# Attention and token/channel mixer on one core: first keys by another queue, a weight ordered by another engine, and a reordered fourth step

## The chip, the core and the metric

The kernel runs on one core of a Trainium2 chip. The core has a matrix engine (TensorE, PE in the profile), a vector engine (VectorE, DVE), a scalar engine (ScalarE, ACT), a general engine (GpSimd, POOL) and a queue engine (SyncE, SP) that here only issues transfers. Each works through its own instructions in the order in which the program lists them, and waits on semaphores where an instruction needs another engine's result. Matmul results go to PSUM, from which VectorE or ScalarE must copy them ("evacuate") to SBUF before they can be used again.

The metric is the device time of one execution in microseconds. A kernel is timed in several runs and the median is compared.

## What is computed

Eight batches of twelve attention heads with 448 tokens and 64 values a head, then a mixer over tokens and one over channels:

```python
scores = scale * np.matmul(q, k.transpose(0, 1, 3, 2))
attn = np.maximum(scores, 0.0) ** 2 / S
x = matmul(attn, v)            # heads joined: (8, 448, 768)
h = np.maximum(x.T @ w_tok1, 0.0) @ w_tok2      # over tokens
u = x + h.T
h2 = np.maximum(u @ w_ch1, 0.0) @ w_ch2         # over channels
out = u + h2
```

Inputs and output are float32. Inside, the kernel works in bf16. The sizes are S = 448, w_tok1 448x256, w_tok2 256x448, w_ch1 768x1536, w_ch2 1536x768.

## The kernel before

**Tiling.** Four heads make a step, so a batch is three steps (DB = 3) and the program has 24 steps (ND = 24). The text calls them step 0, step 1 and so on, by the loop variable i. A step's keys are cut into seven chunks (QC = 7) of 64. All matmuls of scores and values use 64x64 quarters of the array, four at a time.

**One step of attention.** `load_four(i)` (L72) loads queries, keys and values of four heads: two transfers each, issued by GpSimd, which cast from float32 to bf16 on the way. `transposes` (L157) turns queries and keys on TensorE and copies them out as qkT (L181). `scores(i, c)` (L186) makes the scores of a chunk into one of two PSUM tiles, and ScalarE evacuates them with a Relu (L201). `square` (L205) squares them on VectorE (L208). `values(i, cs)` (L210) accumulates the product with the values in ps_acc, which has one tile, and `values_out` (L229) writes it as xT on VectorE (L234).

**Mixer.** `x_back(i)` (L246) turns xT into x_sb: for i below XDMA = 7 by eight TensorE transposes into two PSUM tiles and two VectorE copies (L259, L267), from there on by two DMA transposes issued on SP (L252). `token1` (L271) multiplies by the first token weight, ScalarE evacuates (L284). `token2` (L287) multiplies by the second (L300), and VectorE adds xT into uT (L308). Once a batch has its three steps, `channel_work(b)` (L384) issues the six DMA transposes of `u_back` on SP (L326) and puts units of the channel mixer in a queue: `channel1` is six matmuls and a ScalarE Relu (L338, L345), `channel2` twelve matmuls and a VectorE add (L355, L362), and every second `channel2` unit stores the finished rows (L374). For an even batch the `channel2` units wait until the next batch is done.

**Order.** The program order is written out by hand. The first steps (0 to DB, so 0 to 3) are in a loop over steps and chunks (L432), which places each piece of work after a given chunk. From step 4 on a second loop (L478) is used, and `fill(share)` (L400) takes units from the queue in between: it adds a share of a rate to a credit, and runs units while the credit is above zero, each of which costs its estimated length (C1 = 1134, C2 = 1956). PSUM tiles of the tag "bank" (ps_mm, two of them) are shared by the early transposes, x_back, token1, the early form of token2 and the channel units. In the second loop GpSimd waits by a small copy (`gate`, L493) for x_sb when `i - 1 >= XDMA` before it issues the loads for step i + 3.

**Weights.** All weights are loaded by GpSimd with a cast. The second token weight is loaded in its natural order and rearranged on chip by `order_wt2` (L97): two strided copies of 128x448, one on ScalarE and one on VectorE, placed after chunk 6 of step 1. The first use of it is `token2(0)` in step 2.

**Start.** Nine matmuls on zeros (L417) run while the first loads are on their way. Step 0 has a function of its own for its transposes, `transposes_first` (L121): fourteen transposes for the queries, fourteen for the keys, each 128 partitions high, and copies of their own (L129).

Of the kernel before, what the change touches and what calls it, by code (L numbers as in the profile page):

```python
# [9 lines left out]
FP32 = mybir.dt.float32  # L10
# [6 lines left out]
def kernel(  # L17
# [51 lines left out]


    raws = {}
    def load_four(i):  # L72
        b, d = divmod(i, DB)
        tiles = []
        for name, src in (("q", q), ("k", k), ("v", v)):
            t = raw.tile([128, 2, QC, D], BF16, name=f"{name}_raw")
            for r in range(2):
                h0 = 4 * d + 2 * r
                nc.gpsimd.dma_start(  # L79
                    out=t[64 * r : 64 * (r + 1)].rearrange("p g c d -> p g (c d)"),  # L80
                    in_=src[b, h0 : h0 + 2].rearrange("g (p c) d -> p g (c d)", c=QC),
                )
            tiles.append(t)
        raws[i] = tiles

# [10 lines left out]

    def order_wt2():  # L97
        for j in range(JC):
            (nc.scalar.copy if j == 0 else nc.vector.tensor_copy)(
                wt2[:, j, :].rearrange("n (c p) -> n c p", c=QC),  # L100
                wt2_nat[:, j, :].rearrange("n (p c) -> n c p", c=QC),
            )

    def load_wc1(i, parts):
        n = DC // parts
        nc.gpsimd.dma_start(
            out=wc1[:, :, i * n : (i + 1) * n],
            in_=moe_w_ch1.rearrange("(g p) n -> p g n", p=128)[:, :, i * n : (i + 1) * n],
        )
# [8 lines left out]

    qkT, at2, squares, accs = {}, {}, [], {}

    def transposes_first(i, early=True):  # L121
        sb = attn.tile([128, 2, 2, S], BF16, name="qkT")
        if not early:
            both = ps_acc.tile([128, 2, 1024], BF16, tag="acc", name="qkT_ps")
        def copies(w, ps):
            halves = [slice(0, 2)] if i > 0 or w == 0 else [slice(0, 1), slice(1, 2)]
            for n, r in enumerate(halves):
                on_act = early and (w == 0) == (i > 0) and n == 0
                (nc.scalar.copy if on_act else nc.vector.tensor_copy)(  # L129
                    sb[:, r, w, :].rearrange("n r (c p) -> n r c p", c=QC),  # L130
                    ps[:, : 2 * S].rearrange("n (c r p) -> n r c p", c=QC, r=2)[:, r],
                )

        parts = []
        for w in range(2):
            src = raws[i][w]
            ps = ps_mm.tile([128, 1024], BF16, tag="bank", name="qkT_ps1") if early else both[:, w]
            for c in range(QC):
                for g in range(2):
                    nc.tensor.matmul(  # L140
                        ps[64 * g : 64 * (g + 1), c * 128 : (c + 1) * 128],
                        lhsT=src[:, g, c, :],
                        rhs=ident,
                        is_transpose=True,
                        start=True,
                        stop=True,
                        skip_group_check=True,
                    )
            parts.append(ps)
            if early:  # L150
                copies(w, ps)
        if not early:
            for w in range(2):
                copies(w, parts[w])
        qkT[i] = sb

    def transposes(i, early=False):  # L157
        sb = attn.tile([128, 2, 2, S], BF16, name="qkT")
        if early:
            parts = [ps_mm.tile([128, 1024], BF16, tag="bank", name="qkT_ps1") for r in range(2)]  # L160
        else:
            both = ps_acc.tile([128, 2, 1024], BF16, tag="acc", name="qkT_ps")
            parts = [both[:, r] for r in range(2)]
        for w in range(2):
            src = raws[i][w]
            for c in range(QC):
                at = w * S + c * 64
                for r in range(2):
                    h = slice(64 * r, 64 * (r + 1))
                    for g in range(2):  # L170
                        nc.tensor.matmul(  # L171
                            parts[r][64 * g : 64 * (g + 1), at : at + 64],
                            lhsT=src[h, g, c, :],
                            rhs=ident[h, h],
                            is_transpose=True,
                            start=True,
                            stop=True,
                            skip_group_check=True,
                        )
        for r in range(2):  # L180
            (nc.scalar.copy if early and r == 0 else nc.vector.tensor_copy)(  # L181
                sb[:, r].rearrange("n w t -> n (w t)"), parts[r][:, : 2 * S]
            )
        qkT[i] = sb
# [56 lines left out]


    x_tiles, r1_tiles, uT_tiles = {}, {}, {}
    XDMA = 7

    def x_back(i):  # L246
        b, d = divmod(i, DB)
        x_sb = mix.tile([128, 2, 4, 128], BF16, name="x_sb")
        x_tiles[i] = x_sb
        if i >= XDMA:  # L250
            for r in range(2):
                nc.sync.dma_start_transpose(  # L252
                    out=x_sb[:, r], in_=xT[b % 2][:, 2 * d + r, :]
                )
            return
        for r in range(2):
            ps = ps_mm.tile([128, 1024], BF16, tag="bank", name="x_ps")
            for c in range(4):
                nc.tensor.matmul(  # L259
                    ps[:, c * 128 : (c + 1) * 128],  # L260
                    lhsT=xT[b % 2][:, 2 * d + r, c * 128 : (c + 1) * 128],
                    rhs=ident,
                    is_transpose=True,
                    start=(c == 0),
                    stop=(c == 3),
                )
            nc.vector.tensor_copy(  # L267
                x_sb[:, r], ps[:, :512].rearrange("n (c d) -> n c d", c=4)
            )

    def token1(i):  # L271
        x_sb = x_tiles.pop(i)
# [74 lines left out]
    def channel2(b, t, half):  # L347
# [21 lines left out]
        if half == 1 or last:  # L369
            part = cols if last else slice(0, DM)  # L370
            (b0, c0), (b1, c1) = divmod(2 * t, QC), divmod(2 * t + 1, QC)
            rows = [out[2 * (b // 2) + n].rearrange("(p c) m -> c p m", c=QC) for n in range(2)]
            for k, (n, c) in enumerate(((b0, c0), (b1, c1))):
                nc.sync.dma_start(  # L374
                    out=rows[n][c, :, part], in_=o[64 * k : 64 * (k + 1), part]
                )
        if half == 1:
# [19 lines left out]
    credit = [0.0]  # L397
    rate = [EC * C1 / 3.5]

    def fill(share):  # L400
        if not queue:
            return
        credit[0] += share * rate[0]
        while queue and credit[0] > 0:
            cost, unit = queue.pop(0)
            credit[0] -= cost
            unit()


    PRE = 3  # L410
# [15 lines left out]
    load_wt2()  # L426
    load_four(3)
    load_wc1(0, 2)


    transposes_first(0)
    for i in range(DB + 1):  # L432
        for c in range(QC):
            scores(i, c)
            square(keep=1)
            if c < 3 and i > 0:
                values(i - 1, (4 + c,))
                if c == 2:
                    values_out(i - 1)
            if i < DB:  # L440
                if c == 3:
                    transposes(i + 1, early=True)
                if c == 4 and i > 0:
                    x_back(i - 1)
                if c == 5:
                    values(i, (0, 1))
                if c == 6:
                    if i > 0:
                        token1(i - 1)
                    values(i, (2, 3))  # L450
                if c == 0 and i > 1:
                    token2(i - 2, early=True)
                if c == 6 and i == 1:
                    order_wt2()
            else:
                if c == 0:
                    token2(i - 2, early=True)
                if c == 3:
                    x_back(i - 1)
                if c == 4:  # L460
                    transposes(i + 1)
                    token1(i - 1)
                if c == 6:
                    token2(i - 1)
                    channel_work(0)
        if i == 1:
            load_four(4)
            load_wc1(1, 2)
        if i == 2:
            load_four(5)  # L470
            load_wc2(0, 4)
        if i == 3:
            load_four(6)
            load_wc2(1, 4)
    square()
    fill(1 / 2)

    for i in range(DB + 1, ND + 2):  # L478
        if i == 2 * DB + 1:
# [22 lines left out]
        if i + 1 < ND:  # L502
            transposes(i + 1)
        square()
        fill(1 / 6)
        if 0 <= i - 1 < ND:
            token1(i - 1)
        fill(1 / 6)
        if i < ND:
            scores(i, 5)  # L510
            scores(i, 6)
# [38 lines left out]
```

## Time and profile before

The median of 13 runs is 391.26 us (390.13 to 393.53). The profiled execution took 392.82 us, of which 391.0 lie between its first and last instruction (its span).

| what | value |
|---|---|
| median of 13 runs | 391.26 us |
| profiled execution, span | 392.82 us, 391.0 us |
| granted TensorE clock, mean over the span | 0.977 of full speed |
| TensorE, VectorE, ScalarE, GpSimd busy | 367.9, 207.6, 211.6, 97.9 us |
| chain that ended last, by engine | PE 85%, DVE 5%, DMA 4%, ACT 3% |
| scores' evacuation L201 (168 instructions) | 144.7 us, 920 ns each |
| squares L208 (168) | 97.1 us, 617 ns each |
| loads of q, k, v, issue to landing (median) | 4.2, 5.0, 5.1 us |
| DMA transposes of u and of x, issue to landing (median) | 3.9, 2.4 us |

The profile comes from one execution. Busy time of a matmul engine counts pipelined instructions, so it shows where the engine had work rather than how fast it went. The page divides the span into 40 slices of 9.8 us; a digit is the busy share in tenths. A wait is put down to the engine that released it last.

### The profile page before, as it was taken

How to read it: one execution, taken by the hardware profiler on the slowest of the kernel's cores; microseconds unless marked ns; L12 is line 12 of the kernel's file. 1: busy time of each engine (PE TensorE's matmuls, PEld its weight loads, DVE VectorE, ACT ScalarE, POOL GpSimd, SP SyncE). 2: the span in 40 equal slices, each digit the busy share in tenths (PEclk: the TensorE clock that was granted, in tenths of full speed). 3: DMA queues.
4: the chain of work that ended last, by engine and by line, in shares of the span. 5: the costliest groups of instructions: out<-in, count | busy, mean ns of one | idle time of the engine just before them, and what ended most of it. 6: DMA issues, size and time to landing. Idle time of an engine off the chain costs nothing.

```text
span 391.0 us, 9968 instructions
## 1 busy us (share of the span) xinstructions
PE 367.9 (94%) x4261; PEld 201.0 (51%) x4261; DVE 207.6 (53%) x384; ACT 211.6 (54%) x295; POOL 97.9 (25%) x177
## 2 busy tenths in 40 slices
PE   5877899999999799999999999999999999999995
PEld 2443445445555445555555555545545555555563
DVE  1697676764575635645744756645743755221021
ACT  2987667766644245772676445763576445411400
POOL 9963364510304032223033033123120000000000
PEclk8598999999999989999999999999999999999999
DMA  7999999970359585696557977497453423234024
GB/s 108 131 192 175 181 200 184 183 107 2 57 108 168 94 148 110 102 135 123 109 89 103 119 139 137 78 127 134 113 72 69 89 63 89 59 65 107 2 58 103
DMA packets 70957, 43.33 MB, mean 111 GB/s; under 512 B 44992, under 2 KB 67456, under 8 KB 70912
## 3 DMA queue, kind: packets, MB, share of 16 engines
q0 software_dynamic: 24736, 21.70, 39.1%
q1 hardware_dynamic: 46176, 20.99, 28.1%
q8 instruction: 33, 0.54, 0.6%
q14 instruction: 12, 0.10, 0.1%
HBM read 43.38 MB, written 11.01 MB: 139 GB/s over the span
## 4 chain that ended last, share of the span: by engine, by line
PE 85%; DVE 5%; DMA 4%; ACT 3%; issue 1%; POOL 1%; POOLq 0%; ACTq 0%; DVEq 0%
PE m_ps L355 27%; PE m_ps L338 27%; PE sc_ps L192 9%; PE acc_ps L220 8%; PE t_ps L276 6%; PE h_ps L300 5%; DMA x_sb<-xT 3%; DVE xT L234 3%; PE qkT_ps L171 2%; ACT at L201 2%; DVE at L208 2%; DMA k_raw<-in_k_dram 1%; PE x_ps L259 1%; DVE uT_sb L308 1%; ACT r_sb L284 1%
## 5 line engine op out<-in xcount | busy, mean ns | idle before, releaser
L201 ACT ACTIVATE at<-sc_ps 128x896 bf16<-128x896 f32 x168 | 144.7, 920 | 61.2 <-PE sc_ps L192 61.1
L338 PE MATMUL m_ps<-uT_sb,wc 128*128 128x448 bf16 x576 | 117.4, 353 | 0.5 <-DVE uT_sb L308 0.5
L355 PE MATMUL m_ps<-wc,r_sb 128*128 128x384 bf16 x672 | 116.8, 329 | 0.0
L208 DVE TENSOR_TENSOR at<-at 128x896 bf16<-128x896 bf16 x168 | 97.1, 617 | 6.2 <-ACT at L201 6.2
L345 ACT ACTIVATE r_sb<-m_ps 128x448 bf16<-128x448 f32 x96 | 52.2, 543 | 68.9 <-PE m_ps L338 68.2
L355 PEld LDWEIGHTS <-r_sb 128*128 128x128 bf16 x672 | 64.9, 99 | 46.6 <-issue 5.5
L338 PEld LDWEIGHTS <-wc 128*128 128x128 bf16 x576 | 55.0, 98 | 50.9 <-issue 3.4
L362 DVE TENSOR_TENSOR out_sb<-m_ps,u_sb 128x384 f32<-128x384 f32 x56 | 31.0, 553 | 61.7 <-PE m_ps L355 61.7
L192 PE MATMUL sc_ps<-qkT 64*64 64x448 bf16 x672 | 54.4, 373 | 3.0 <-ACT at L201 2.3
L308 DVE TENSOR_TENSOR uT_sb<-h_ps,xT 128x448 bf16<-128x448 f32 x48 | 27.7, 619 | 53.4 <-PE h_ps L300 53.4
L234 DVE TENSOR_SCALAR xT<-acc_ps 128x448 bf16<-128x448 f32 x48 | 27.7, 619 | 32.3 <-PE acc_ps L220 32.3
L493 POOL COPY gate<-x_sb 1x1 bf16<-1x1 bf16 x13 | 2.5, 196 | 148.6 <-DMA x_sb<-xT 148.6
L220 PE MATMUL acc_ps<-at,v_raw 64*64 64x448 bf16 x672 | 39.6, 359 | 0.0
L79 POOL DMA_DIRECT2D q_raw<-in_q_dram x48 | 28.9, 609 | 26.9 <-DMA wc<-in_moe_w_ch_dram 18.6
L181 DVE COPY qkT<-qkT_ps 128x896 bf16<-128x896 bf16 x43 | 24.9, 619 | 17.6 <-PE qkT_ps L171 17.6
L192 PEld LDWEIGHTS <-qkT 64*64 64x64 bf16 x672 | 15.5, 107 | 31.5 <-issue 27.3
L79 POOL DMA_DIRECT2D v_raw<-in_v_dram x48 | 29.4, 635 | 6.1 <-PE sc_ps L192 4.3
L79 POOL DMA_DIRECT2D k_raw<-in_k_dram x48 | 29.1, 623 | 4.2 <-DMA k_raw<-in_k_dram 1.9
L276 PE MATMUL t_ps<-x_sb,wt 128*128 128x256 bf16 x192 | 25.7, 278 | 2.8 <-DMA x_sb<-xT 2.8
L284 ACT ACTIVATE r_sb<-t_ps 128x512 bf16<-128x512 f32 x24 | 14.4, 599 | 22.4 <-PE t_ps L276 22.4
L220 PEld LDWEIGHTS <-v_raw 64*64 64x64 bf16 x672 | 20.1, 109 | 12.5 <-issue 1.2
L300 PE MATMUL h_ps<-wt,r_sb 128*128 128x448 bf16 x96 | 22.3, 355 | 1.7 <-ACT r_sb L284 1.0
(35 smaller groups left out, 103.2 us busy)
## 6 DMA issues: line engine op xcount, KB each, us to landing
out_dram<-out_sb SPq DMA_DIRECT2D x54, 192.0 KB, 2.7
q_raw<-in_q_dram POOLq DMA_DIRECT2D x48, 112.0 KB, 4.2
k_raw<-in_k_dram POOLq DMA_DIRECT2D x48, 112.0 KB, 5.0
v_raw<-in_v_dram POOLq DMA_DIRECT2D x48, 112.0 KB, 5.1
wc<-in_moe_w_ch_dram POOLq DMA_DIRECT2D x2, 1152.0 KB, 14.0
wc<-in_moe_w_ch_dram POOLq DMA_DIRECT2D x4, 576.0 KB, 11.1
u_sb<-uT_sb SPq DMA_TRANSPOSE x48, 3.9
x_sb<-xT SPq DMA_TRANSPOSE x34, 2.4
```

Of the source, the lines that this page charges most:

```text
L79: nc.gpsimd.dma_start(out=t[64 * r : 64 * (r + 1)].rearrange("p g c d -> p g (c d)"), in_=src[b, h0 : h0 + 2].rearrange("g (p c) d -> p g ...
L192: nc.tensor.matmul(ps[64 * r : 64 * (r + 1), g, :S], lhsT=sb[h, r, 1, c * 64 : (c + 1) * 64], rhs=sb[h, r, 0, :], start=True, stop=True, s ...
L201: nc.scalar.activation(at, ps[:, :, :S], AF.Relu)
L208: nc.vector.tensor_tensor(out=at, in0=at, in1=at, op=ALU.mult)
L220: nc.tensor.matmul(ps[64 * g : 64 * (g + 1), r, :S], lhsT=v_raw[h, g, c, :], rhs=at[h, g, :], start=(c == 0), stop=(c == QC - 1), skip_gro ...
L234: nc.vector.tensor_scalar(out=xT[b % 2][:, 2 * d + r, :S], in0=ps[:, r, :S], scalar1=float(alpha2), scalar2=None, op0=ALU.mult,)
L276: nc.tensor.matmul(ps[:, j, :], lhsT=wt1[:, c, j * 128 : (j + 1) * 128], rhs=x_sb[:, :, c, :], start=(c == 0), stop=(c == 3),)
L300: nc.tensor.matmul(parts[r][:, :S], lhsT=r1[:, j, r * 128 : (r + 1) * 128], rhs=wt2[:, j, :], start=(j == 0), stop=(j == JC - 1),)
L308: nc.vector.tensor_tensor(out=uT_tiles[b // 2][:, 2 * d + r, off : off + S], in0=parts[r][:, :S], in1=xT[b % 2][:, 2 * d + r, :S], op=ALU.add,
L338: nc.tensor.matmul(ps[:, :S], lhsT=wc1[:, g, e * 128 : (e + 1) * 128], rhs=uT[:, g, off : off + S], start=(g == 0), stop=(g == CC - 1),)
L345: nc.scalar.activation(r2[:, e, off : off + S], ps[:, :S], AF.Relu)
L355: nc.tensor.matmul(ps[:, :HN], lhsT=r2[:, e, t * 128 : (t + 1) * 128], rhs=wc2[:, e, cols], start=(e == 0), stop=(e == EC - 1),)
```

## The change

The diff has seven parts.

1. For step 0, the two transfers of the keys are issued on SP and on ScalarE's queue instead of GpSimd's, as float32 into a new tile `k_first`. One ScalarE copy and one VectorE copy cast its halves to bf16.
2. `order_wt2` is called after the issue of the first half of the first channel weight, ahead of step 0, and both its copies are on GpSimd.
3. `transposes_first` is gone. Step 0 uses `transposes(0, early=True)`, which turns the keys before the queries for this step. ScalarE copies out one pair of heads (128x896), VectorE the other.
4. `x_back` puts its eight transposes into one PSUM tile, with one copy out of it, and XDMA goes from 7 to 6: step 6's x goes by DMA transposes, and GpSimd's gate begins in step 7.
5. In step 3 (i = DB) the last values of step 2 come ahead of the scores of chunks 0 and 1, and x_back, token1, token2 and the channel work move up by one or two chunks. token2 takes its early form (ps_mm). One `fill(1 / 4)` runs after chunk 5 and one after the loop, instead of one `fill(1 / 2)` after the loop.
6. In the second loop the shares around token1 are 2/9 and 1/9 instead of 1/6 and 1/6, and the second takes at least one unit.
7. The second of the two transfers at each of the last two stores is issued on ScalarE's queue.

```diff
+    k_first = consts.tile([128, 2, QC, D], FP32, name="k_first")
     def load_four(i):
...
-                nc.gpsimd.dma_start(
-                    out=t[64 * r : 64 * (r + 1)].rearrange("p g c d -> p g (c d)"),
+                eng, dst = nc.gpsimd, t
+                if i == 0 and name == "k":
+                    eng, dst = (nc.sync, nc.scalar)[r], k_first
+                eng.dma_start(
+                    out=dst[64 * r : 64 * (r + 1)].rearrange("p g c d -> p g (c d)"),
...
+            if i == 0 and name == "k":
+                nc.scalar.copy(t[:, 0], k_first[:, 0])
+                nc.vector.tensor_copy(t[:, 1], k_first[:, 1])
...
     def order_wt2():
         for j in range(JC):
-            (nc.scalar.copy if j == 0 else nc.vector.tensor_copy)(
+            nc.gpsimd.tensor_copy(
...
-    def transposes_first(i, early=True):
...
     def transposes(i, early=False):
...
-        for w in range(2):
+        for w in (1, 0) if i == 0 else (0, 1):
...
-    XDMA = 7
+    XDMA = 6
     def x_back(i):
...
+        ps = ps_mm.tile([128, 2, 512], BF16, tag="bank", name="x_ps")
         for r in range(2):
-            ps = ps_mm.tile([128, 1024], BF16, tag="bank", name="x_ps")
             for c in range(4):
                 nc.tensor.matmul(
-                    ps[:, c * 128 : (c + 1) * 128],
+                    ps[:, r, c * 128 : (c + 1) * 128],
...
-            nc.vector.tensor_copy(
-                x_sb[:, r], ps[:, :512].rearrange("n (c d) -> n c d", c=4)
-            )
+        nc.vector.tensor_copy(
+            x_sb.rearrange("n r c d -> n (r c d)"), ps.rearrange("n r t -> n (r t)")
+        )
...
-                nc.sync.dma_start(
+                (nc.scalar if last and k else nc.sync).dma_start(
...
-    def fill(share):
+    def fill(share, least=0):
...
-        while queue and credit[0] > 0:
+        done = 0
+        while queue and (credit[0] > 0 or done < least):
             cost, unit = queue.pop(0)
             credit[0] -= cost
             unit()
+            done += 1
...
     load_wc1(0, 2)
-    transposes_first(0)
+    order_wt2()
+    transposes(0, early=True)
     for i in range(DB + 1):
         for c in range(QC):
+            if i == DB and c < 2:
+                square()
+                values(i - 1, ((4,), (5, 6))[c])
+                if c == 1:
+                    values_out(i - 1)
             scores(i, c)
             square(keep=1)
-            if c < 3 and i > 0:
+            if c < 3 and 0 < i < DB:
                 values(i - 1, (4 + c,))
...
-                if c == 6 and i == 1:
-                    order_wt2()
             else:
                 if c == 0:
                     token2(i - 2, early=True)
+                if c == 2:
+                    x_back(i - 1)
                 if c == 3:
-                    x_back(i - 1)
+                    token1(i - 1)
                 if c == 4:
                     transposes(i + 1)
-                    token1(i - 1)
-                if c == 6:
-                    token2(i - 1)
+                    token2(i - 1, early=True)
                     channel_work(0)
+                if c == 5:
+                    fill(1 / 4)
...
-    fill(1 / 2)
+    fill(1 / 4)
...
-        fill(1 / 6)
+        fill(2 / 9)
         if 0 <= i - 1 < ND:
             token1(i - 1)
-        fill(1 / 6)
+        fill(1 / 9, least=1)
```

## The prediction

> **What bounds the kernel now.** I read the engines' shares first, then the slices, then the chain of waits, and last the order of time around each place that the change touches.
>
> ```profile
> PE 367.9 (94%) x4261; PEld 201.0 (51%) x4261; DVE 207.6 (53%) x384; ACT 211.6 (54%) x295; POOL 97.9 (25%) x177
> PE   5877899999999799999999999999999999999995
> PEclk8598999999999989999999999999999999999999
> ```
>
> TensorE is busy nearly everywhere, except in the first six slices (59 us) and in one slice near 130 us. A slice is 9.8 us. So a saving counts only if it lies in the first steps, in a gap of TensorE later on, or at the very end. In 10 to 20 us ScalarE is busy 9.32 of 10 us and the granted clock is 0.61; in 20 to 30 us VectorE has 9.05 and ScalarE 8.91, while TensorE has 6.57. The first two steps are evacuation work, not matmul work.
>
> The chain of waits, at its start:
>
> ```profile
> 1.44 1.32 POOL q_raw L79 x2
> 2.77 0.55 POOL k_raw L79
> 3.32 4.41 DMA k_raw<-in_k_dram
> 7.86 0.97 PE qkT_ps L140 x14
> 8.86 0.54 ACT qkT L129
> 9.45 1.02 PE sc_ps L192 x4
> ```
>
> The columns are start, length, and what. The first keys land at 7.73 us, behind the queries in GpSimd's issues of 0.6 us each; the first scores begin at 9.45.
>
> Among the waits, the lines that this change bears on (total, times, longest):
>
> ```profile
> ACT qkT L129 <- PE qkT_ps L140: 6.6, 1, 6.6
> ...
> PE x_ps L259 <- DVE xT L234: 3.0, 5, 0.8
> ...
> PE h_ps L300 <- ACT r_sb L284: 1.0, 4, 0.2
> ...
> PE h_ps L300 <- ACT wt L99: 0.7, 1, 0.7
> ```
>
> **1. First keys by hardware queues.** Removed: two GpSimd issues (2.74 to 3.90 us), so everything behind them on that queue is issued 1.16 us earlier. Added: one issue on SP, idle then, from about 0.75; one on ACT behind the table load and the gate activation, which end at 2.24; two casts of 128x448. The first scores now need 56 small transposes instead of 14 behind the last arrival, and a copy of 128x896 on ACT instead of 128x448. No hardware load of fp32 is in this trace; the nearest row is the output store, 192 KB, 2.7 us from issue to landing. The keys' halves read 229 KB each (twice the page's 112 KB, which counts bf16), so by bytes about 3.2 us: ACT's half lands at 2.24 + 3.2 = 5.45. The queries landed at 2.10 + 2.9 = 5.0; I give them 0.3 for sharing. Then: cast 0.54 (the ACT copy of 128x448 took 0.53) to 6.0; both groups of transposes 1.0 (at half clock 28 took 0.63 and 0.56, partly overlapping) to 7.0; ACT copy 0.93 to 7.95; scores at 8.05. Gain **1.4 us**. The Trainium skill (DMA: Bandwidth & Descriptors, Rules for kernel authors) speaks against this: spreading DMAs over issuers gives no bandwidth since all share 16 engines, and two transfers to disjoint partition halves serialize. If so, both tensors land when the same bytes landed before, less the issue time: 7.73 - 1.2 = 6.5, and with 0.54, transposes of the keys 0.5 and queries 0.5, copy 0.93, scores come at 9.0: gain 0.45. But the row shows the engines with a DMA share of 0.00 in 1 to 2 us and 0.15 in 2 to 3: SP's half moves in empty time. I take 1.4; ends 0 and 2.4 (ACT issues ahead of its activation, at about 1.2).
>
> This gain holds through steps 0 and 1, where ACT works without gaps. Next late would be the keys of step 2: issued at 14.05 and 14.66, 4.3 to landing, so 19.0 before and 17.8 now, against a need of 19.4 before and 18.0 now. It just holds.
>
> **2. GpSimd orders the second token weight.** Removed from step 1: ACT 0.91 (0.79 of the chain) and DVE 0.87. TensorE waited 0.67 for it, so h_ps at 25.85 could have begun at 25.18; with part 1 at 23.8. Now the copies are on GpSimd behind the issue of the first channel weight. They can start when the weight has landed: 16.38 + 6.3 = 22.7 before, 21.5 now. No such GpSimd copy is in the trace. Nearest rows: the select on 128x128 took 0.29 us, by elements 1.0 us for 448; the same strided copy took 0.87 on DVE and 0.91 on ACT, so 0.9 is the low end. The Trainium skill (GPSIMD Engine Reference, Performance pitfalls for Q7 kernels, and Key points) states about 2.9 cycles an element at 1.2 GHz when the step exceeds 8 bytes (here 7 x 2 = 14): 1.1 us plus the 0.2 of a tiny GpSimd copy, and contention with VectorE instructions of two SBUF inputs, which the squares are, in a stretch where VectorE is full. By the rows 2 x 1.0 ends at 23.5 and hides; by the rule 2 x 1.4 ends at 24.3. I take the rule, as the row's input is not strided: h_ps at 24.4, **1.45 us** earlier than 25.85. So of parts 1 and 2 only 1.45 survives together, and a poorer start costs nothing until h_ps without order would pass 24.4. High end 3.5 us a copy: h_ps at 28.6, 2.8 us later than before. Queued behind the copies on GpSimd is step 4's load (first issue at 23.23 before, 24.3 now). The keys of step 4 landed at 36.8 and were needed at 40.3; the DMA share is over 1.1 there, so bytes and not the issue set the landing. Covered, with some 2 us to spare.
>
> **3. The x transposes share one bank.** In steps 1 and 2 x_ps waited 1.60 us each for a VectorE evacuation, though ScalarE's bank was free 0.4 earlier. One bank instead of two may save 0 to 0.4 each; I take 0.2 in all. In steps 4 to 6 the wait is for xT and remains; one copy of 1,024 for two of 512 changes nothing on the path.
>
> **4. Values of step 2 ahead of the fourth step's scores.** The values move two slots up, but VectorE's queue decides: uT of step 1 (36.34 to 37.50), a square, then xT. It starts at about 38.0 instead of 38.53, so token1 is 0.5 earlier too. Then it is given back: transposes now precede token2, so two qkT copies (1.15) run ahead of uT, and token2 takes both ps_mm banks, so the first channel unit (43.48 before, with a bank free) waits for the first uT copy, about 44.0. Net 0.2; ends -0.8 and 1.0.
>
> **5. Fill.** I worked out the units per slot (after x_back, before token1, after token1, after token2). Before, step 4 has 1,1,0,2; step 5: 1,0,1,1; step 6: 1,1,0,1; step 8: 2,2,0,2. After: 1,1,1,1; 1,1,1,0; 1,1,1,0; 2,2,1,1. The wait of 0.25 for r_sb goes in steps 4, 6 and 8: 0.75. But in steps 5 and 6 nothing lies between token2 and the next scores. In order of time, ScalarE and TensorE in step 5:
>
> ```profile
> 66.88 1.72 ACT L201 ACTIVATE at<-sc_ps 128x896 bf16<-128x896 f32 x2
> ```
> ```profile
> 67.61 1.30 PE L338 MATMUL m_ps<-uT_sb,wc 128*128 128x448 bf16 x6
> 68.84 0.57 PE L192 MATMUL sc_ps<-qkT 64*64 64x448 bf16 x8
> ```
>
> The unit (1.14 us) covers the evacuation until 68.60. Without it scores could go at 67.7, but the second needs the bank freed at 68.60, so values start about 0.75 late. Cost 2 x 0.75 = 1.5. Sum of the part: **-0.75**.
>
> **6. x_back(6) by DMA transpose.** In step 7:
>
> ```profile
> 81.24 0.36 PE L192 MATMUL sc_ps<-qkT 64*64 64x448 bf16 x4
> 82.14 0.93 PE L259 MATMUL x_ps<-ident,xT 128*128 128x128 bf16 x8 [0.55 <-DVE xT L234]
> 83.06 3.57 PE L338 MATMUL m_ps<-uT_sb,wc 128*128 128x448 bf16 x18
> ```
>
> The idle 0.55 and the 0.93 go: **1.5 us**. SP has two u_back transposes just before (79.14 to 82.35), then two of 1.2 us; landing by 83.6 + 2.8 = 86.4 against token1 at about 88.3. Step 10's load now waits on this through the gate: about 14 us later than at 72.4, needed at 116. Covered.
>
> **7. Last store.** SP issues the last two in turn, 0.56 us each; on ACT, idle then, the second goes beside the first: **0.5**.
>
> Sum: 1.45 + 0.2 + 0.2 - 0.75 + 1.5 + 0.5 = **3.1 us**. Against the profiled span of 391.0: 387.9, and with the 1.8 around it (392.82 in all) 389.7. The median of the runs shown is 391.26, 1.56 below that run; the clock dips (0.50 at 31.4 to 34.6; 0.57 at 137 to 141) may differ by run. I apply the gain to the median: **388.2**.
>
> **Rivals.**
> *Slower by x_back(6).* In step 10 the transposes sat behind u_back on SP: TensorE waited 2.07 us, then 12 matmuls took 3.63 instead of 1.95 at the lower clock. The same in step 7 makes 3.7 lost instead of 1.5 gained: 391.26 + 2.1 = 393.4. It decides once x_sb lands over 1.9 us later than I reckon. For it: same place in the cycle of three steps; casting loads, which stretched u_back's landing to 8.8. Against: two u_back transposes ahead here, six there, and the next load is held back by the gate. With GpSimd's high end of 3.5 us a copy instead, the sum is 3.1 - 4.2 = -1.1: about 392.4. Together 0.13.
> *No change.* The stalls of part 5 reach 1.2 each, part 4 loses 0.8, parts 1 and 2 bring 0.9: 3.1 - 0.9 - 1.0 - 0.5 = 0.7, so 390.5. For it: three edits hand their gain to the same VectorE and ScalarE queues. 0.16.
> *More.* GpSimd copies at 1.0 and the dip at 31 to 35 gone: about 386.5. 0.10.
> *Forecast* 388.2, own range 386.9 to 390.0: 0.61.
>
> The bound of telling is 0.3%, 1.2 us. Faster 0.71, same 0.16, slower 0.13. The range runs 386.2 to 391.4: it leaves out most of the slower cases and little below.
>
> **What would show it.** First scores at 8 us; two GpSimd copies of 1.4 us ending near 24.3 with h_ps just behind; no wait of h_ps for r_sb after step 3; waits of sc_ps for ACT at the ends of steps 5 and 6; m_ps straight after scores in step 7 and no wait of token1 for x_sb there. Wrong if GpSimd's copies take over 2.5 us each, or if step 7 shows a DMA wait.

## The result, and the profile after

The changed kernel took 387.04 us (median of 11 runs, 384.85 to 389.06) against 391.49 us for the kernel before (48 runs): a ratio of 0.9891, with a 95% interval of 0.9866 to 0.9917, or 4.3 us (3.2 to 5.2). The profiled execution has a span of 385.2 us against 391.0.

The page of the changed kernel, engines and slices as before:

```profile
PE 364.8 (95%) x4281; PEld 199.8 (52%) x4281; DVE 205.7 (53%) x375; ACT 212.6 (55%) x295; POOL 100.0 (26%) x178
...
PE   6696898999999799999999999999999999999995
...
PEclk9869999999999999999999999999999999999999
```

TensorE's first slices are fuller, the clock no longer drops near 137 us (slice 15), and the hole of slice 14 is still there. The start, in order of time (start, length, engine, line, what; "ACTq" and "SPq" issue transfers):

```profile
0.74 0.74 SPq L83 DMA_DIRECT2D k_first<-in_k_dram  x1
...
1.18 0.72 ACTq L83 DMA_DIRECT2D k_first<-in_k_dram  x1
...
5.21 0.56 ACT L88 CAST k_raw<-k_first 128x448 bf16<-128x448 f32 x1 [2.97 <-DMA k_first<-in_k_dram]
...
5.83 0.41 PE L142 MATMUL qkT_ps<-ident,k_raw 64*64 64x64 bf16 x28 [0.61 <-ACT k_raw L88]
...
6.52 0.91 ACT L152 COPY qkT<-qkT_ps 128x896 bf16<-128x896 bf16 x1 [0.74 <-PE qkT_ps L142]
...
7.48 0.57 PE L163 MATMUL sc_ps<-qkT 64*64 64x448 bf16 x8 [1.01 <-ACT qkT L152]
```

ACT issues its half at 1.18, while its table load still runs (0.74 to 2.02) and ahead of the activation at 2.03 that stands before it in the program: the order described above for an engine's instructions does not hold for the issue of a transfer. The first scores start at 7.48 instead of 9.45. Of the waits, these lines are the ones to compare, first of the kernel before and then of the changed one:

```profile
PE t_ps L276 <- DMA x_sb<-xT: 2.8, 3, 2.1
...
PE sc_ps L192 <- ACT at L201: 2.3, 6, 0.6
```
```profile
PE sc_ps L163 <- ACT at L172: 3.6, 9, 0.8
...
PE t_ps L248 <- DMA x_sb<-xT: 2.1, 1, 2.1
...
PE qkT_ps L142 <- DMA k_raw<-in_k_dram: 1.2, 2, 0.9
```

In this execution the waits of h_ps for r_sb and for the ordered weight are gone. Scores now wait longer for ScalarE, TensorE waits 1.2 us for the keys of step 2, and of three waits for x_sb the one of step 10 stays.

To see where 5.8 us of span went, I took from both traces the start of each step's values (TensorE writing acc_ps) and compare the stretches between them:

```
stretch                            before   after   difference
start to values of step 3           47.06   45.38     -1.68
step 3 to 4                         11.81   11.35     -0.46
step 4 to 5                         10.37   11.13     +0.76
step 5 to 6                         10.68   11.16     +0.48
step 6 to 7                         17.17   15.69     -1.48
step 7 to 8                         15.02   14.70     -0.32
step 8 to 9                         13.29   13.29      0.00
step 9 to 10                        19.10   17.48     -1.62
step 10 to 11                       14.20   13.89     -0.31
step 11 to the end of the last add 228.44  227.78     -0.66
from there to the end of the span    3.86    3.35     -0.51
```

One row is not of the change. Between the values of steps 9 and 10, TensorE waits for x_sb in both (2.07 and 2.12 us); before, the twelve matmuls behind the wait took 3.79 us at a dropped clock, now 2.11. Without that row 4.2 us are left. That this is close to the 4.3 of the timing is partly chance, since it compares one execution with one.

The first row hides a second clock drop. Granted clock (the column before the DMA share) from 19 to 26 us, in the changed kernel and then in a later run with XDMA = 7, which has the same program up to there:

```profile
19.00:26.00 7.00, 6.47 (x50) 3.10 (x50) 3.58 (x6) 4.69 (x6) 5.79 (x8) 0.52 1.20 191
```
```profile
19.00:26.00 7.00, 5.69 (x103) 3.07 (x103) 6.78 (x10) 5.52 (x8) 6.00 (x9) 1.00 1.20 193
```

Twice the matmuls in the same time. The kernel before was at half clock from 7.5 to 17.7 and from 31.4 to 34.8 us, the changed kernel from 8.7 to 12.1 and from 19.0 to 25.8. So the trace of a single execution says little about the start; the runs below say more.

### The profile page after: what moved, and what is told of

Read it like the earlier page. It is cut to its first block, busy times and chain, and to the rows that moved or that the text cites. A ratio compares the mean times of both kernels' runs of the same rounds, so it can differ in the third digit from the quotient of the medians.

```text
span 385.2 us, 10018 instructions
## 1 busy us (share of the span) xinstructions
PE 364.8 (95%) x4281; PEld 199.8 (52%) x4281; DVE 205.7 (53%) x375; ACT 212.6 (55%) x295; POOL 100.0 (26%) x178
## 3 DMA queue, kind: packets, MB, share of 16 engines
HBM read 43.38 MB, written 11.01 MB: 141 GB/s over the span
## 4 chain that ended last, share of the span: by engine, by line
PE 85%; DMA 8%; POOL 3%; DVE 1%; issue 1%; ACT 1%; POOLq 0%; ACTq 0%
PE m_ps L310 29%; PE m_ps L327 28%; PE sc_ps L163 8%; PE acc_ps L191 7%; PE t_ps L248 5%; PE h_ps L272 4%; DMA q_raw<-in_q_dram 4%; DMA wc<-in_moe_w_ch_dram 3%; PE qkT_ps L142 2%; POOL q_raw L83 1%; POOL v_raw L83 1%; DVE xT L205 1%; DMA x_sb<-xT 1%; POOL wt L97 1%; POOL k_raw L83 1%
## 5 line engine op out<-in xcount | busy, mean ns | idle before, releaser
L327 PE MATMUL m_ps<-wc,r_sb 128*128 128x384 bf16 x672 | 115.2, 326 | 0.0
L163 PE MATMUL sc_ps<-qkT 64*64 64x448 bf16 x672 | 53.4, 369 | 4.8 <-ACT at L172 3.6
L473 POOL COPY gate<-x_sb 1x1 bf16<-1x1 bf16 x14 | 3.3, 236 | 151.2 <-DMA x_sb<-xT 151.2
L163 PEld LDWEIGHTS <-qkT 64*64 64x64 bf16 x672 | 15.7, 106 | 33.1 <-issue 29.5
L83 POOL DMA_DIRECT2D k_raw<-in_k_dram x46 | 27.9, 623 | 4.6 <-issue 1.9
L248 PEld LDWEIGHTS <-wt 128*128 128x128 bf16 x192 | 18.9, 100 | 9.5 <-issue 4.2
```

The lines of the kernel that those rows point to most:

```text
L83: eng.dma_start(out=dst[64 * r : 64 * (r + 1)].rearrange("p g c d -> p g (c d)"), in_=src[b, h0 : h0 + 2].rearrange("g (p c) d -> p g (c d ...
L163: nc.tensor.matmul(ps[64 * r : 64 * (r + 1), g, :S], lhsT=sb[h, r, 1, c * 64 : (c + 1) * 64], rhs=sb[h, r, 0, :], start=True, stop=True, s ...
L248: nc.tensor.matmul(ps[:, j, :], lhsT=wt1[:, c, j * 128 : (j + 1) * 128], rhs=x_sb[:, :, c, :], start=(c == 0), stop=(c == 3),)
L327: nc.tensor.matmul(ps[:, :HN], lhsT=r2[:, e, t * 128 : (t + 1) * 128], rhs=wc2[:, e, cols], start=(e == 0), stop=(e == EC - 1),)
```

## The experiments

Ratios are to the kernel before; the changed kernel has 0.9891. An interval is about 0.003 to 0.004 to each side, so differences below some 1.5 us are read from the traces.

### u_keys: first keys by GpSimd again

```diff
-                if i == 0 and name == "k":
-                    eng, dst = (nc.sync, nc.scalar)[r], k_first
...
-        for w in (1, 0) if i == 0 else (0, 1):
+        for w in range(2):
```

> The changed kernel with its first keys loaded by GpSimd with the cast again (and the queries transposed first), all else kept. Theory (the keys start the work earlier, but the keys of step 2 land late and take back part): first scores at about 9.4 us instead of 7.5; the keys of step 2 are issued two GpSimd issues later and land about 0.7 later than the 18.3 of the changed kernel, so step 2's transposes end about 0.7 later and only that much reaches step 4, 0.7 to 1.2 us. Time about 388.0, 0.2 to 0.3% slower than the changed kernel. Rival (the whole shift of the first scores is worth its size): 2.0 us or more at step 4, about 389.0. Rival (the issuing queue is worth nothing since all share the same engines): first scores within 0.5 of 7.5.

Measured: 389.12 us, ratio 0.9948 (0.9917 to 0.9979). First scores at 9.10, against 7.48 to 8.43 where the part is kept:

```profile
9.10 0.96 PE L158 MATMUL sc_ps<-qkT 64*64 64x448 bf16 x8 [0.96 <-ACT qkT L147]
```

Values of step 3 start at 44.51, with a clock of 1.0 up to there; where the keys come by hardware queues, the loads keep the changed kernel's order and the clock held from 16 to 35 us, they start at 43.03 (u_xdma), 43.50 (u_fill), 43.53 (f_fill), 43.78 (u_step3) and 44.27 (f_fill_ub_late). The part is worth 0.2 to 1.5 us at that point; the timing says 2.2 with an error of 1.6. Another 0.75 us of this run lies in step 7 (see u_fill). The issuing queue does matter here, against the third theory: in the changed kernel SP's transfer moves from 2.3 us on, in this run the first GpSimd transfer from 2.9. What the queue does, what leaving the cast to an engine does, and what the order of the first transposes does is not separated.

### u_order: the second token weight by ScalarE and VectorE again

```diff
-            nc.gpsimd.tensor_copy(
+            (nc.scalar.copy if j == 0 else nc.vector.tensor_copy)(
...
-    order_wt2()
...
+                if c == 6 and i == 1:
+                    order_wt2()
```

> The changed kernel with the second token weight ordered by ScalarE and VectorE after step 1's last scores again. Theory (GpSimd's copies, 2.5 us from 22.2, are hidden, and the 0.8 us that they take from ScalarE is worth what ScalarE is short of there): h_ps of step 2 begins 0.3 to 0.9 later than 25.6 at the same granted clock, time about 387.6. Rival (GpSimd's copies hold h_ps and the load of step 4 back): h_ps begins at the same time or earlier, step 4's queries are issued about 1 us earlier than 24.6, time 387.0 or less. Rival (the granted clock decides): if TensorE is at full clock between 20 and 25 us in this execution, h_ps begins earlier than 25.6 whatever orders the weight.

Measured: 387.92 us, ratio 0.9907 (0.9873 to 0.9941): not told apart from the changed kernel. Its profiled execution has two clock drops (20 to 24 and 30 to 34 us), so its trace does not answer either; the question was put again as g_order.

### u_fill: the old shares

```diff
-        fill(2 / 9)
+        fill(1 / 6)
...
-        fill(1 / 9, least=1)
+        fill(1 / 6)
```

> The changed kernel with the shares 1/6 and 1/6 around token1 and no least unit, as before. Theory (the new placing costs at the ends of steps 5 and 6 and gains elsewhere): sc_ps waits for ACT vanish at the ends of steps 5 and 6, 0.75 and 0.5 us regained there; h_ps waits of 0.25 for r_sb come back in steps 4, 6 and 8; token1 waits for x_sb again in steps 11 and 20 (0.3 and 0.6 in the trace of before). Sum about 0.2 to 0.6 slower than the changed kernel, within what the timing can tell. Rival (the stalls at steps 5 and 6 are all that counts): 0.8 us faster than the changed kernel, 386.2.

Measured: 388.10 us, ratio 0.9943 (0.9914 to 0.9971). The stretches from step 4 to 5 and 5 to 6 are 10.22 and 10.53 us instead of 11.13 and 11.16: 1.54 regained. The stretches 3 to 4 and 7 to 8 lose 0.32 and 0.31. From the values of step 10 to the last add it takes 242.76 us instead of 241.66, 1.10 more, and token1 waits 0.39 and 0.13 us for x_sb in steps 18 and 21; the first theory had two such waits. The largest loss is in step 7, 17.90 us instead of 15.69, and neither theory had it. Step 7, in order of time on TensorE:

```profile
82.03 2.44 PE L310 MATMUL m_ps<-uT_sb,wc 128*128 128x448 bf16 x12
86.56 1.03 PE L248 MATMUL t_ps<-x_sb,wt 128*128 128x256 bf16 x8 [2.08 <-DMA x_sb<-xT]
```

and transfers between 76 and 90 us, first of this run and then of the changed kernel (last column: us from issue to landing):

```profile
u_sb<-uT_sb SPq DMA_TRANSPOSE x2, 9.0
x_sb<-xT SPq DMA_TRANSPOSE x2, 7.0
```
```profile
u_sb<-uT_sb SPq DMA_TRANSPOSE x2, 2.4
x_sb<-xT SPq DMA_TRANSPOSE x2, 2.4
```

This is the prediction's slower rival, in part. Step 6's x goes by DMA transposes while the casting loads of step 9 are still in the queues. The last of these, first of this run and then of the changed kernel:

```profile
76.87 1.18 POOL L83 DMA_DIRECT2D v_raw<-in_v_dram  x2 [2.33 <-DMA k_raw<-in_k_dram]
```
```profile
71.12 1.19 POOL L83 DMA_DIRECT2D v_raw<-in_v_dram  x2
```

They landed at 85.6 and at 80.5 us, while step 6's values came at 75.9 and 79.0. So the step was earlier and the loads were later. The lateness of the loads counts for more: they landed at 84.5 to 85.6 us in u_fill, f_fill, u_keys and f_k2, where x_sb landed within 1.7 us behind them and token1 waited 2.08, 1.87, 0.59 and 0.60 us; they landed by 82.7 at the latest in u_order, u_step3, f_ub and the changed kernel, where it did not wait. Yet u_keys and f_k2 had step 6's values at 78.1 and 77.9, later than u_step3 with 77.4. (In u_keys and f_k2 the profile puts the wait down to ScalarE, but x_sb landed last, 0.13 to 0.14 us before token1.) Why GpSimd came so late to these loads in some runs is not shown.

### u_xdma: XDMA at 7 again

```diff
-    XDMA = 6
+    XDMA = 7
```

> The changed kernel with XDMA at 7, so step 6's x goes by TensorE transposes again and GpSimd's gate begins a step later. Theory: in step 7 an idle of 0.55 and the transposes' 0.93 come back between scores and the channel unit; values of step 7 begin 1.5 us later after those of step 6 (17.2 instead of 15.7 us), time about 388.5, 0.4% slower than the changed kernel. Rival (the step was hidden by the evacuations at its ends): under 0.5 us.

Measured: 389.01 us, ratio 0.9952 (0.9921 to 0.9982). In step 7 the gap is back:

```profile
77.99 0.39 PE L163 MATMUL sc_ps<-qkT 64*64 64x448 bf16 x4
78.92 0.93 PE L230 MATMUL x_ps<-ident,xT 128*128 128x128 bf16 x8 [0.54 <-DVE xT L205]
79.68 3.57 PE L310 MATMUL m_ps<-uT_sb,wc 128*128 128x448 bf16 x18
```

In the changed kernel the channel matmuls follow the scores at once:

```profile
80.34 0.39 PE L163 MATMUL sc_ps<-qkT 64*64 64x448 bf16 x4
80.66 3.58 PE L310 MATMUL m_ps<-uT_sb,wc 128*128 128x448 bf16 x18
```

The stretch from step 6 to 7 is 17.05 us instead of 15.69: 1.36 us, about what the theory says; the timing says 2.4 with an error of 1.6.

### u_step3: step 3 as before

```diff
-            if i == DB and c < 2:
-                square()
-                values(i - 1, ((4,), (5, 6))[c])
...
-                    token2(i - 1, early=True)
+                if c == 6:
+                    token2(i - 1)
...
-    fill(1 / 4)
+    fill(1 / 2)
```

> The changed kernel with step 3 as before: last values behind the scores, x_back after chunk 3, token1 after chunk 4, token2 in ps_acc and the channel work after chunk 6, one fill of 1/2 behind the loop. Theory (the new order of step 3 hands its gain back to VectorE's queue and to the shared PSUM tiles): from the first h_ps of step 3 (token2 of step 1) to the first scores of step 4 it takes within 0.5 us of the changed kernel's 10.9; time within 0.7 us of 387.0. Rival (the new order is worth 1 us or more, as the earlier x_back and token1 free the end of the step): 1 us or more longer in that stretch, about 388.2 or more.

Measured: 386.38 us, ratio 0.9875 (0.9835 to 0.9916). From token2 of step 1 to the first scores of step 4 it takes 10.89 us (32.49 to 43.38); the changed kernel takes 10.98 (33.99 to 44.97), the kernel before 10.91 (35.75 to 46.66). The whole reordering of step 3 brings nothing. In the changed kernel:

```profile
40.46 1.16 DVE L152 COPY qkT<-qkT_ps 128x896 bf16<-128x896 bf16 x2 [0.73 <-PE qkT_ps L142]
...
41.53 1.14 DVE L280 TENSOR_TENSOR uT_sb<-h_ps,xT 128x448 bf16<-128x448 f32 x2
...
42.19 1.30 PE L310 MATMUL m_ps<-uT_sb,wc 128*128 128x448 bf16 x6 [0.60 <-DMA q_raw<-in_q_dram]
```

The two qkT copies run ahead of uT, and the first channel unit starts at 42.19, just behind uT's first copy (41.53 + 0.6). The releaser that the last line names, a load of queries, is inferred; neither the unit's operands nor its bank come from it.

### f_fill and f_fill_late: a unit behind token2 in steps 5 and 6, and the last quarter of the second channel weight later

```diff
-        fill(2 / 9)
+        fill(0 if i in (5, 6) else 2 / 9)
...
-        fill(1 / 9, least=1)
+        fill(1 / 3 if i in (5, 6) else 1 / 9, least=1)
```

and, in f_fill_late as well,

```diff
+            if i == 2 * DB + 1:
+                load_wc2(3, 4)
             load_four(i + PRE)
-        if i in (4, 5):
+        if i == 4:
```

> The changed kernel with its unit in front of token1 in steps 5 and 6 moved behind token2 (shares 0 and 1/3 there instead of 2/9 and 1/9), so each of these steps again has a unit between token2 and the next scores. Theory (what is saved at steps 5 and 6 is taken back in step 7, as token1 there waits for x_sb, whose DMA transposes lie behind the casting loads of step 9): sc_ps no longer waits 0.43 for ACT at the ends of steps 5 and 6, values of step 6 come about 1.2 us earlier than those of step 4 would give in the changed kernel; but x_sb of step 6 takes 5 to 7 us to land and token1 waits 0.5 to 2 us; time 386.0 to 388.0. Rival (the stalls are simply removed): no wait in step 7, 385.8.

> As f_fill, and the last quarter of the second channel weight is loaded behind the gate of step 7 instead of in step 5, so that 1.18 MB fewer are queued ahead of step 9's loads. Theory (step 7's stall is the loads' queue): x_sb of step 6 lands within 3 us of its issue, token1 of step 7 doesn't wait, time about 385.8. Rival (the DMA transposes are slow for another reason): token1 waits as in f_fill.

Measured: f_fill 385.05 us, ratio 0.9856 (0.9813 to 0.9900); f_fill_late 385.11 us, ratio 0.9848 (0.9806 to 0.9889). The timing does not separate them from each other, and f_fill's time lies below the 386.0 to 388.0 of its theory; the traces do separate them. In both, steps 4 to 6 take 20.44 us instead of 22.29: 1.85 us gained. In f_fill step 7 takes it back, 17.69 us instead of 15.69:

```profile
85.74 1.03 PE L248 MATMUL t_ps<-x_sb,wt 128*128 128x256 bf16 x8 [1.87 <-DMA x_sb<-xT]
```
```profile
x_sb<-xT SPq DMA_TRANSPOSE x2, 6.7
```

In f_fill_late step 7 takes 15.66 us and nothing waits for x_sb:

```profile
83.64 2.44 PE L310 MATMUL m_ps<-uT_sb,wc 128*128 128x448 bf16 x12
85.93 1.04 PE L248 MATMUL t_ps<-x_sb,wt 128*128 128x256 bf16 x8
```
```profile
x_sb<-xT SPq DMA_TRANSPOSE x2, 2.4
```

One caution: its start had a clock drop, so step 6's values came at 77.5 us, 2.2 later than in f_fill, which alone would ease the collision. The combined kernels below, with values of step 6 at 75.5 to 76.1, have no wait either, and u_fill with 75.9 has one. In f_fill_late and the combined kernels step 9's values landed at 77.6 to 80.4 us, in f_fill at 84.5, which makes the loads' queue the cause.

### f_ub: u_back in two parts

```diff
+            b, d = divmod(i - 1, DB)
+            if d == DB - 1 and b > 1:
+                u_back(b, range(4))
...
-        u_back(b)
+        u_back(b, range(4 if b > 1 else 0, NP))
```

> The changed kernel with u_back split from the third batch on: its first four DMA transposes go right behind x_back of the same step, the last two behind token2, so two instead of six lie ahead of the next step's x_back on SP. Theory (the wait of 2.1 us in step 10 is SP's issue time of 1.25 us for each of six transposes): token1 of step 10 no longer waits for x_sb; 2.1 us faster than the changed kernel, 385.0; where the granted clock dropped behind that wait, up to 1.7 more. Rival (the transposes land late because of other transfers): the wait stays at over 1 us.

Measured: 384.59 us, ratio 0.9836 (0.9798 to 0.9874). SP's queue around step 10, in the changed kernel:

```profile
120.82 7.95 SPq L298 DMA_TRANSPOSE u_sb<-uT_sb  x6
128.88 3.25 SPq L223 DMA_TRANSPOSE x_sb<-xT  x2
```

and with the split:

```profile
122.19 2.54 SPq L299 DMA_TRANSPOSE u_sb<-uT_sb  x2
124.83 2.52 SPq L223 DMA_TRANSPOSE x_sb<-xT  x2
```

The stretch from step 9 to 10 is 15.24 us instead of 17.48. Six transposes at 1.3 us of issue each had held x_sb up; the theory holds. Of the ten kernels profiled with that wait (the first two, and all runs above and below without the split), five show a dropped clock at its end or behind it (19.1 to 20.3 us in that stretch) and five do not (17.5 to 17.7). Four of the five with a drop had waits of 2.60 to 3.40 us, the fifth, the kernel before, one of 2.07; the five without had 2.12 to 2.38. The four profiles with the split show neither the wait nor a drop.

### f_k2: keys of step 2 ahead of the first token weight

```diff
+    load_four(2, "qk")
     load_wt1()
-    load_four(2)
+    load_four(2, "v")
```

> The changed kernel with queries and keys of step 2 issued on GpSimd ahead of the seven loads of the first token weight instead of behind them. Theory (behind the earlier first scores, the keys of step 2 are what is late: TensorE waited 1.2 us for them in the changed kernel's trace): the keys' transposes of step 2 follow the queries' without a wait, ScalarE has no idle before qkT of step 2, and step 4's values come 0.3 to 1.0 us earlier than the 43.0 to 43.8 of the executions whose clock didn't drop between 16 and 35 us; time about 386.5. Rival (the second token weight or the clock sets h_ps of step 2 anyway): keys no longer waited for, but step 4's values as before, time 387.0. Rival (the first token weight becomes late): token1 of step 1 waits for it.

Measured: 388.17 us, ratio 0.9920 (0.9893 to 0.9948). The keys are no longer waited for, the first token weight isn't either, and step 2's first uT starts at 23.66 us, against 23.89 to 25.13 without this edit at a held clock (u_xdma, f_ub, u_fill, f_fill, u_step3, f_fill_ub_late): 0.2 to 1.5 us. The kernel as a whole is no faster, where 386.5 was expected; its trace has 0.6 us lost ahead of token1 in step 7 (see u_fill), 2.7 in step 10, and a clock drop behind that. Alone the edit is inconclusive.

### f_fill_ub_late, f_all and g_order: the mends together

The first has the edits of f_fill_late and f_ub, f_all has f_k2's as well, and g_order is f_all with the weight ordered as before.

> The changed kernel with the three mends together: a unit behind token2 in steps 5 and 6, the last quarter of the second channel weight behind step 7's gate, u_back split from the third batch on. Theory (each removes its own stall, on TensorE's path): 1.2 + 2.2 = 3.4 us off the changed kernel, about 383.5, ratio to the kernel before about 0.980; no wait of token1 for x_sb. Rival (one stall covers for the other): 384.6, no better than the split alone.

> As f_fill_ub_late, with queries and keys of step 2 ahead of the first token weight. Theory: 0.3 to 1.0 us better than f_fill_ub_late, about 383.0. Rival: the same within 0.3.

> As f_all, with the second token weight ordered by ScalarE and VectorE after step 1's last scores again. Theory (ScalarE is short in step 1, so 0.8 us comes back): with an undropped clock h_ps of step 2 begins 0.5 to 0.8 later than in f_all, and step 4's values 0.3 to 0.8 later, time 0.5 us above f_all. Rival (GpSimd's copies hold the second half of h_ps as long as ScalarE's would): h_ps ends within 0.3 of f_all's, time equal to f_all's.

Measured: 383.05 us, ratio 0.9795 (0.9761 to 0.9829); 381.22 us, 0.9754 (0.9729 to 0.9778); 382.60 us, 0.9790 (0.9754 to 0.9826). f_all beats both kernels; its interval lies wholly below the changed kernel's. Its lead over f_fill_ub_late, 1.8 us, is larger than expected but not clear of the intervals. The stalls did not cover for each other. No wait of token1 for a DMA transpose of x is left.

f_all and g_order ran nearly the same clock up to 29 us, so the pair answers u_order. TensorE and the copies, f_all first:

```profile
21.35 2.10 POOL L107 COPY wt<-wt_nat 128x448 bf16<-128x448 bf16 x2
...
23.26 0.60 ACT L257 ACTIVATE r_sb<-t_ps 128x512 bf16<-128x512 f32 x1 [0.69 <-PE t_ps L249]
...
24.04 0.93 PE L273 MATMUL h_ps<-wt,r_sb 128*128 128x448 bf16 x4
```
```profile
23.21 0.60 ACT L257 ACTIVATE r_sb<-t_ps 128x512 bf16<-128x512 f32 x1 [0.69 <-PE t_ps L249]
...
23.71 0.88 ACT L107 COPY wt<-wt_nat 128x448 bf16<-128x448 bf16 x1
...
24.64 0.92 PE L273 MATMUL h_ps<-wt,r_sb 128*128 128x448 bf16 x4 [0.58 <-ACT wt L107]
```

GpSimd's copies end at 23.45, before h_ps needs them; ScalarE's copy ends at 24.59 and holds it 0.58 us. That is the part's worth where the clock is low around 21 us. The 1.4 us between the two times are not clear of the intervals. In the traces step 2's first uT starts at 24.63 and 25.21, values of step 3 at 43.76 and 45.90; the rest of that difference, 1.56 us, goes with a half clock at 29.7 to 33.1 us in g_order alone.

## Why the prediction was right

**The whole.** The forecast was 3.1 us off the median, the timing says 4.3 (3.2 to 5.2). Parts 1, 2, 6 and 7 have the right sign and about the right size. Part 4 brought nothing, part 5 has the wrong sign over the whole kernel, and no run takes part 3 out. Put together from the runs below, parts 1 to 3 bring 1.3 to 2.5 us, part 4 -0.1, part 5 0.2, part 6 1.4 to 1.5 where no load is in its way, part 7 0.4 to 0.5: by this estimate 3.1 to 4.6. What the forecast surely lacks is part 5's gain in the later steps; how much the start adds to that can't be read from the traces, whose clocks differ.

**Part 1** was somewhat small at the first scores, which came 1.0 to 2.0 us earlier, at 7.5 to 8.4 in the traces (reckoned: 8.05). The keys landed at 5.0 to 5.4 us (reckoned: 5.45), as ACT issued ahead of its activation, which the prediction had as an end; the queries landed late, at 6.0 to 6.8 (reckoned: 5.3). The skill's rule that spreading issues gives no bandwidth but only saves issue time (Trainium skill, DMA: Bandwidth & Descriptors, Rules for kernel authors) would have given 9.0 as the prediction reckoned it; the row of the empty engines was the better guide, and u_keys shows the difference. The sharing that the rule speaks of is in the traces too: the queries land at 5.0 in the kernel before and in u_keys. What was named as next late, the keys of step 2, did not always hold. In the changed kernel they landed at 17.7 and 18.3 instead of 17.8 at the latest, because GpSimd's queue, which waited 0.62 us for another transfer, gained only 0.63 of its 1.16, and TensorE waited 1.25 us for them; in u_fill and u_xdma the queue gained 1.25 to 1.36 and TensorE waited 0.36.

**Part 2** had the right mechanism and too long copies: 1.7 to 2.6 us for both, mostly 2.1 to 2.5, where 2.8 was taken. A copy beside an idle VectorE took 0.87 us (f_fill_ub_late), less than the rule that the prediction followed makes of it and nearer to its rows; beside squares up to 1.36 (u_keys). The second half of h_ps waits for them where the clock holds (0.28 us in u_xdma, 0.87 in u_fill). These are the copies, h_ps and uT in u_xdma and, with the keys on GpSimd, in u_keys:

```profile
21.33 2.11 POOL L106 COPY wt<-wt_nat 128x448 bf16<-128x448 bf16 x2 [1.00 <-DMA wt_nat<-in_moe_w_tok_dram]
...
23.50 0.73 PE L272 MATMUL h_ps<-wt,r_sb 128*128 128x448 bf16 x3 [0.28 <-POOL wt L106]
...
23.89 1.16 DVE L280 TENSOR_TENSOR uT_sb<-h_ps,xT 128x448 bf16<-128x448 f32 x2
```
```profile
22.34 2.59 POOL L101 COPY wt<-wt_nat 128x448 bf16<-128x448 bf16 x2 [0.82 <-DMA wt_nat<-in_moe_w_tok_dram]
...
24.98 0.73 PE L267 MATMUL h_ps<-wt,r_sb 128*128 128x448 bf16 x3 [0.26 <-POOL wt L101]
...
25.36 1.16 DVE L275 TENSOR_TENSOR uT_sb<-h_ps,xT 128x448 bf16<-128x448 f32 x2
```

In all seven such executions with a clock of 1.0 from 16 to 28 us (these two, u_fill, u_step3, f_fill, f_ub, f_fill_ub_late) uT starts 0.44 us after the copies end, and the values of step 3 start 19.0 to 19.2 us after that uT (20.7 in f_ub, where the clock drops at 28.8). So what reaches step 3 is not the earlier first scores but the landing of the second token weight, 21.1 to 23.0 us in the six with the keys on hardware queues (reckoned: 21.5) and 22.3 in u_keys, and the time of the copies. Of part 1, GpSimd's two saved issues are what counts there. Step 2's first uT started at 23.89 to 25.13 in these six, against 26.42 before: 1.3 to 2.5 us for parts 1 to 3, where the sum had 1.45 + 0.2. The changed kernel's own trace shows 26.25, since its clock was half there, and the kernel before's dropped later.

**Part 4**: 0.2 predicted, -0.1 by u_step3, for the reason given: VectorE's queue and the shared banks.

**Part 5**: -0.75 predicted. From old to new shares (u_fill against the changed kernel), steps 4 and 8 gain 0.32 and 0.31 and steps 5 and 6 lose 0.91 and 0.63: -0.91. But the steps from 11 on gain 1.10, to which the prediction gave nothing, so the part brings about 0.2. It did not see that the extra unit ahead of token1 also hides x_sb landing late: the kernel before waited 0.25 and 0.45 us for it in steps 11 and 21, u_fill 0.39 and 0.13 in steps 18 and 21, the changed one doesn't.

**Part 6**: 1.5 predicted, 1.48 in the trace and 1.36 by u_xdma. The slower rival was closer than its 0.13 says: its mechanism, casting loads that stretch the transposes' landing, took 2.08 us in u_fill, 1.87 in f_fill and 0.6 in u_keys and f_k2, four of the eight kernels that were profiled with XDMA = 6 and without f_fill_late's edit of the loads. The prediction set the landing at 86.4 with the loads gone and named the gate against the rival; but the gate holds back step 10's loads, and those in the way are step 9's. That the changed kernel's trace shows the full gain is in part luck: its start ran at half clock and part 5 delayed steps 5 and 6, so step 7 came late, and the loads were early.

**Part 7**: 0.5 predicted, 0.51 between the two traces and 0.4 to 0.5 over all runs.

## What to carry to other kernels

A saving at the start of a pipelined kernel is spent at the next transfer that was just in time: look not only for the next wait but for each later place where compute now meets a queue that has not moved (here the second token weight, and step 9's loads). Filler work belongs where an in-order engine would wait for an evacuation, so place it by the wait it covers rather than by equal shares. Before judging a start by one trace, compare its granted clock, for a dropped stretch can hide or feign 1.5 us and more.

## What the runs showed of the hardware that was not expected

The clock drops are not a property of the kernel: executions of the same opening program had a half clock at 8.7 to 12.1 and 19.0 to 25.8 us (the changed kernel), at 7.6 to 14.4 us only (f_fill_ub_late), or none before 133 us (u_fill, u_xdma). Up to 375 us into a trace a drop lasted 3.41 us or two or three times that. One of 3.41 us between 28 and 35 us cost 1.5 us: from step 2's first uT to the values of step 3 it took 20.6 to 20.7 us with it (five traces) and 19.0 to 19.2 without (nine). In step 10 all four waits of 2.60 to 3.40 us came with a drop, and one of the six of 2.07 to 2.38; what decides it is not shown.

GpSimd's strided copies and VectorE's squares slow each other: both copies took 1.67 us where VectorE was idle (f_fill_ub_late) and up to 2.59 beside squares (u_keys), and a square beside them took 1.30 us (f_all) and up to 1.90 (f_k2) instead of 0.62. They behave as if they took turns: a square that began during a copy ended about 0.5 us after the end of that copy (in f_k2, of both copies), and a copy that began during a square ended about 0.75 us after the end of that square. This agrees with what the Trainium skill (GPSIMD Engine Reference, Key points) says of VectorE instructions with two SBUF inputs.
